# Grouping the narrow products of a fused filter, feed-forward and slot-routing kernel on one core

## The chip, the core and the metric

One core of a Trainium2 chip runs the whole program. The metric is device time in microseconds of one execution. The kernel before takes 1836.76 us (median of three runs, 1835.94 to 1837.98).

## What is computed

Three layers follow each other on x of 8 x 3072 x 256, all in float32:

```python
X = np.fft.rfft(x, axis=1); Y = X * (filt_r + 1j * filt_i)
x = np.fft.irfft(Y, n=3072, axis=1).reshape(24576, 256)     # filter
h = np.maximum(x @ w_in, 0.0); x = h * h @ w_out            # 256 -> 2048 -> 256
logits = x @ phi                                            # 32 slots, 4 for each of 8 experts
d = softmax(logits, axis=0); slot_in = d.T @ x              # over all 24576 rows
slot_out = relu(slot_in @ w1[e]) @ w2[e]                    # per expert
out = softmax(logits, axis=1) @ slot_out
```

## The kernel before, in words

The 24576 rows go through the feed-forward layer in 48 chunks of 512 rows, six to a batch. A chunk is eight pairs; a pair is two 128-wide tiles of the hidden layer, each made by six full 128 x 128 products of 512 columns (`layer`, L594 to L596, into the PSUM banks `p0` and `p1`), then squared (`square`, L601, L603, L605) and turned (`turn_h`, L622). Time in the hand-written order counts in units of half a pair: a chunk is 16 units, and pair P runs from unit 2P to 2P + 2. `pair` fires, quarter by quarter, whatever stands in five lists (`dsp`, `mv`, `late`, `fft`, `w`, in this order) with a unit that has come. Functions that need PSUM banks wait for their turn until enough of five side banks (`s0` to `s4`) are free (`run_streams`, `takes`).

"Narrow" products use a part of the array, several at a time. There are six kinds:

- the logits (`logit`, L663, 128 x 32), fired by `pair` itself at units 1.5 and 9.5 of a chunk: 16 instructions each time
- the slots product of the chunk before (`slot_in`, L794, 128 x 32, 32 instructions) at unit 9.5, added into a running sum by `accum` (L855, L856)
- the inverse transform over n1 of the rows of the next chunk (`mm_y`, L514, 64 x 64, 64 instructions) at unit 9.5, then `even_y` (L522), `unfold` (L531), `lead_y` (L539) and `rest_y` (L546)
- the forward transform over n1 of a later batch (`mm_a`, L165, 64 x 64, 16 instructions, three per batch)
- the forward transform over n2 (`mm_b`, L299, 48 x 32, 64 instructions, four per batch), then the filter (`filt`, L310) and `join` (L319)
- the inverse over n2 (`mm_g2`, L218, 32 x 64, 64 instructions, four per batch), then `evac_g2` and `store_g2`

The first three stand in one stretch at unit 9.5: logits, slots, inverse over n1. The last three are placed by the table `when` (the units of `mm_a`, `mm_b` and `mm_g2` of a batch) and their loads by the table `LEAD`. In a batch from the fourth on, `mm_g2` and one `mm_a` stand at units 1.5 (behind the logits), one `mm_b` as well, and three `mm_b` and two `mm_a` stand at unit 6, alone among full products. All loads and stores but a few go through SP's queue in the order written. The last batches' transforms are done before the last six chunks.

Ahead of the chunks lies an opening of some 55 us (its own put list, `put0`): batch 0's transforms with the x loads (`load_u`), the conversion of 64-bit weights on VectorE (`conv`), and the first input tile `gi`. Behind them lies the expert stage and the output loop (L1403 to L1423), 48 steps that write 512 KB each.

Of the kernel before, what the change touches and what calls it, by code (L numbers as in the profile page):

```python
# [6 lines left out]
F32 = mybir.dt.float32  # L7
# [6 lines left out]
NB = 8  # L14
# [24 lines left out]
def body(tc, x, cA, cAf, fwp, fwd, ivp, inv, flt, cst, w_in, w_out, phi, w1, w2, out):  # L39
# [23 lines left out]
    def F(i):  # L63
        return ST["F0"] + ST["dF"] * i

    WI = [
        ([.26, .3], [[9.7, 9.9, 9.91, 9.92, 9.93, 9.94], [12.9, 13.3, 13.31, 13.32, 13.33, 13.34]], 20.4, 40.3),
        ([.35, .425], [[16.6, 17.1, 17.11, 17.12, 17.13, 17.14], [30.2, 40.4, 40.41, 40.42, 40.43, 40.44]], 47.2, 47.58),
        ([30.1], [[41, 46, 46.1, 46.2, 46.3, 46.4]], 47.3, W + .1),
# [5 lines left out]
         + [W + t for t in (7.45, 7.95, 7.5, 8, 8.95, 9)]),  # L75
        (W + 5.2, [W + 9.3, W + 9.6, W + 10.2, W + 11, W + 11.5, W + 12.1]
         + [W + t for t in (13.95, 14.45, 14, 14.5, 15.45, 15.5)]),
# [43 lines left out]


    def fft_events(b, pl, put, TA, TB, TG, n, st):
        xv = x[b].rearrange("(p n) d -> p n d", n=N2)
# [21 lines left out]

        def load_u(u):
            sl, n = divmod(2 * u, 4)
            st["x", sl] = st["big"][sl // 4][:, sl % 4]
            sync.dma_start(out=st["x", sl][:, n:n + 2], in_=xv[:, 2 * u:2 * u + 2, :])  # L150

# [203 lines left out]
        def store_g(i):  # L355
# [4 lines left out]
            for r in range(2):  # L360
                (act if i == 6 and r else sync).dma_start(
                    out=gv[i % 6, r], in_=st["go", i][64 * r:64 * r + 8]
                )

        def store_rest(nm, lo, hi):
# [10 lines left out]
        def load_ca():  # L376
            vec.memset(st["wz"], 0.0)
            act.dma_start(out=st["ca"], in_=cAf)
# [8 lines left out]
        if b == 0:  # L387
# [8 lines left out]
            for u in range(12):  # L396
                put((.2, .21, .22, .23, .24, .25, .27, .28, .29, .31, .33, .34)[u], load_u, u)
            put(.32, load_k, C_ID, C_SS)
            put(.46, load_k, C_I, C_ID)
# [9 lines left out]
            for i in range(8):  # L409
                put((.38, .4, .42, .44)[i] if i < 4 else F(i - 4) + 2.6, load_f, i)  # L410
                T = (16.8, 17.2, 20, 22.4, 24.9, 25.3, 27.4, 27.8)[i]
                for s in range(2):
                    put(T + .1 * s, mm_t, i, s)
                    put(T + .3 + .1 * s, evac_t, i, s)
                put(F(i) - 1.2, mm_b, i)
                for r in range(2):
                    put(F(i) + 1.25 * r, filt, i, r)
                    if i < 7:
                        put(F(i) + 1.3 + 1.25 * r, join, i, r)
                put((29.85, 32.3, 34.75, 37.2, 39.9, 41.5, 44.6, 40.5)[i], mm_g, i)  # L420
                T = (31.1, 33.6, 36.1, 38.6, 41.2, 44.7, 45.9, 42.4)[i]
                for c in range(4):
                    put(T, evac_g, i, c)
                put(T + 1.25, store_g, i)
            return

        for s, (TL, TF, T) in enumerate(TA):
            put(TL, load_x, s)
            for k in range(2):
                put(TF + k, fold_x, s, k)  # L430
                for g in range(2):
                    put(T + 0.5 + (0 if T % 16 == 6 else 0.5) * k, evac_a, s, k, g)
                put(T + 2 + 0.5 * k, store_a, s, k)
            put(T, mm_a, s)
        LW, LV, LF, LS = n["lead"]
        for j in range(4):
            T = TB[j]
            for k in range(2):
                i = 2 * j + k
                put(T - LW[j], load_w, i)  # L440
                put(T, mm_b, i)
                for r in range(2):
                    put(T + 0.5 + 2 * k + r, filt, i, r)
                    put(T + 1 + 2 * k + r, join, i, r)
# [4 lines left out]
            put(T, mm_g2, j)  # L449
            for c in range(4):  # L450
                put(T + 0.5 + 0.5 * (c // 2), evac_g2, j, c)
            put(T + 3, store_g2, j)

    def out_events(b, st, late):

        def load_g(g):
            if b + g:
                t = G["mlp"].tile([128, 4, D], F32, tag="gin", name="gin", bufs=2)
                src, o = (st["G1"], 0) if (b, g) == (0, 1) else (st["G"], 4 * g - 8 * (b == 0))
                sync.dma_start(out=t, in_=src[:, o:o + 4, :])  # L460
            else:
                t = scratch("gi", 1, [128, 4, D])
                sync.dma_start(out=t[0:96], in_=st["Gu"])
                sync.dma_start(out=t[96:128], in_=st["Gz"])
            st["gi", g] = t

# [37 lines left out]
        def mm_y(g):  # L504
            t = st["gi", g]
            st["y", g] = p = [side() for e in range(2)]
            for a in range(4):
                for k in range(2):
                    for e in range(2):
                        for d in range(2):  # L510
# [6 lines left out]
                                start=True, stop=True, skip_group_check=True, tile_position=(64 * e, 64 * d),  # L517
                            )

        def even_y(g):  # L520
# [27 lines left out]
        for g in range(NCB):  # L548
            if 6 * b + g not in (0, 1, 6):
                T = 96 * b + 16 * g - 6.5  # L550
                late(max(T - 19.5, 13.5), load_g, g)
                late(T, mm_y, g)
                late(T + 0.5, even_y, g)
                late(T + 1, unfold, g, ALU.add)
                late(T + 1, unfold, g, ALU.subtract)
                for k in range(2):
                    late(T + 2 + 2 * k, lead_y, g, k)
                    late(T + 2.5 + 2 * k, rest_y, g, k)
                continue
# [138 lines left out]
    def dispatch_events(c, put):  # L698
# [87 lines left out]
        def slot_in():  # L786

            st["S"] = S = side()
            e, h = st["eT"], hd.pop(c)
            for t in range(4):  # L790
                for n in range(4):
# [4 lines left out]
                        start=(t == 0), stop=(t == 3), tile_position=(0, 32 * n),  # L796
                    )

        def slot_blocks():
# [91 lines left out]
        else:  # L891
# [3 lines left out]
            put(q + 4, expo)  # L895
            put(q + 4, turn_l)
            put(q + 5, rescale)
# [5 lines left out]
        else:  # L903
            put(q + 7.5, slot_in)
            put(q + 9, accum)
        put(q + 11, row_max)
# [47 lines left out]
    def conv(key, k, part=slice(0, 1024)):  # L954
# [11 lines left out]
        if k < 5:  # L966
            wst["s", key].pop(0)()
        else:
            e = gps if key[0] == "o" and key[1] else vec
            e.tensor_tensor(out=a, in0=a, in1=wst["e", key].bitcast(F32), op=ALU.add)  # L970

# [60 lines left out]
    def takes(fn, a):  # L1032
        if fn is conv_wo and a[1] in (6, 7, 10):
            return 1
        return take.get(fn.__name__, 0)

# [72 lines left out]
    with tc.manual_schedule():  # L1109
# [25 lines left out]
        for n in range(4):  # L1135
# [4 lines left out]
        LEAD = [  # L1140
            [[6.5, 6.5, 9.5, 9.5], [10, 7.5, 8, 10], [5, 6, 6.5, 6.5], [5.5, 10.5, 10, 10]],
            [[5.5, 7.5, 15.25, 15.25], [6.5, 12.5, 13.5, 13.5], [5, 5.5, 10, 10], [5.5, 13, 15.25, 15.25]],
            [[20.25] + [15.25] * 3, [13.5] * 4, [20.5, 10, 10, 10], [8, 15.25, 15.25, 15.25]],
        ]
# [8 lines left out]
        for b in range(1, NB):  # L1153
            st = {}
            if b == 1:
                when = ([(22, 24.5, 26.5), (24, 29, 33.5), (27.5, 32, 36.5)], [47, 54.5, 65.5, 76.5], [53, 61.5, 70.5, 81.5])
            elif b == 2:
                when = ([(-19, -15.5, -10), (-11, -7, -3), (-5.5, -3, 0)], [13.5, 22, 38, 54], [18.5, 33.5, 49.5, 65.5])
            else:
                when = ([(-41, -31, -26), (-28, -22.5, -14.5), (-22.5, -15.5, -10)], [1.5, 22, 38, 54], [17.5, 33.5, 49.5, 65.5])  # L1160
            fft_events(b, lambda: G["fft"], stream("fft", 96 * (b - 1)), *when, dict(f=3, u=8, c=2, lead=LEAD[min(b, 3) - 1]), st)
            out_events(b, st, late)
# [239 lines left out]

        obs = [w1t[n][:, 4 * D * h:4 * D * (h + 1)] for n in range(1, 5) for h in range(2)]  # L1403
        ops = 0
        for g in range(NG):
            b, o = divmod(g, N2 // 4)
            ov = out[b * N:(b + 1) * N, :].rearrange("(p n) d -> p n d", n=N2)
            ct = cts.pop(g)
            ob = obs[g % len(obs)].rearrange("p (a d) -> p a d", d=D)
            for h in range(2):  # L1410
                p = bank(("s0", "s1", "s2", "s3")[ops % 4]).rearrange("p (a d) -> p a d", d=D)
                ops += 1
                for a in range(2):
                    pe.matmul(p[:, a, :], ct[:, 2 * h + a, :], sr, start=True, stop=True)  # L1414
                if h == 0:
                    act.activation(out=ob[:, 0:2, :], in_=p, func=ACTF.Copy)
                else:
                    vec.tensor_copy(ob[:, 2:4, :], p)
                if g == 0:
                    sync.dma_start(out=ov[:, 2 * h:2 * h + 2, :], in_=ob[:, 2 * h:2 * h + 2, :])  # L1420
            if g:
                sync.dma_start(out=ov[:, 4 * o:4 * o + 4, :], in_=ob)
                go(*((turn, stack) if g == 1 else (turn, keep, stack)))  # L1423
# [154 lines left out]
```

## Time and profile before

| | us |
|---|---|
| median of three runs | 1836.76 |
| the profiled execution | 1835.65 |
| its span, first to last instruction | 1833.9 |
| PE busy | 1804.7 (98%) |
| VectorE, ScalarE, GpSimd busy | 1199.4, 1035.1, 781.2 |
| DMA queue of SP, share of 16 engines | 79.3% |

A row of the timeline gives the start in us from the span's start, the length, the engine, the line in the source, the tiles and how many instructions are merged. Matmuls overlap by their pipeline, so the time that one takes is read from start to start and not from its length. A row of the windows gives, for a stretch, the busy time of each engine with its instructions, the granted TensorE clock, the busy share of the DMA engines and GB/s.

### The profile page before, as it was taken

The page shows a single profiled execution, that of the slowest core. Times are in us where ns is not written, and L with a number is a line of the kernel's source. Part 1 is how long each engine was busy: PE and PEld are TensorE (multiplying, and loading weights), DVE is VectorE, ACT ScalarE, POOL GpSimd, SP SyncE. Part 2 cuts the span into 40 slices and gives each one's busy share as a digit, 9 for nine tenths or more (in the row PEclk, how much of TensorE's full clock was granted, in tenths as well). Part 3 has the DMA queues.
Part 4 walks back from the last instruction along what each step waited for, and adds up shares of the span by engine and source line. Part 5 has one row for each costly group of instructions (what it writes and reads, how often), then busy time and mean ns, then how long its engine had stood idle before and what let it go on. Part 6 is the DMA issues. An engine that isn't in the chain of part 4 may idle for free.

```text
span 1833.9 us, 42128 instructions
## 1 busy us (share of the span) xinstructions
PE 1804.7 (98%) x16326; PEld 1192.0 (65%) x16326; DVE 1199.4 (65%) x2264; ACT 1035.1 (56%) x1930; POOL 781.2 (43%) x815
## 2 busy tenths in 40 slices
PE   9999999999999999999999999999999999999986
PEld 7666666666666666666666666666666676666555
DVE  7956666676666666666667666666576756565568
ACT  6755555555555564555655565556555565555545
POOL 4144553444444534544444444444354533333234
PEclk9999999999999999999999999999999999999999
DMA  9779889888877896887978798788878666675989
GB/s 314 214 186 279 259 234 259 258 223 227 248 213 200 227 275 182 232 238 211 260 210 222 204 259 230 194 234 222 259 201 234 193 179 176 171 205 151 304 307 378
DMA packets 239846, 425.03 MB, mean 232 GB/s; under 512 B 25888, under 2 KB 95136, under 8 KB 239648
## 3 DMA queue, kind: packets, MB, share of 16 engines
q1 hardware_dynamic: 238776, 421.13, 79.3%
q8 instruction: 130, 2.13, 0.5%
q10 hardware_dynamic: 728, 1.15, 0.2%
q14 instruction: 68, 0.56, 0.1%
q0 software_dynamic: 144, 0.07, 0.0%
HBM read 151.71 MB, written 77.59 MB: 125 GB/s over the span
## 4 chain that ended last, share of the span: by engine, by line
PE 95%; DVE 2%; issue 1%; DMA 1%; ACT 1%; POOL 0%; SPq 0%; ACTq 0%; DVEq 0%; POOLq 0%
PE p L594 21%; PE p L596 19%; PE p L595 19%; PE L L663 10%; PE sd L794 9%; PE sd L299 3%; PE sd L218 3%; PE sd L514 3%; PE sd L165 2%; DVE ct L1212 1%; PE pt L1201 1%; PE sd L265 1%; PE pt L1414 1%; PE sd L339 1%; PE sd L724 1%
## 5 line engine op out<-in xcount | busy, mean ns | idle before, releaser
L605 POOL TENSOR_TENSOR h<-h 128x512 f32<-128x512 f32 x375 | 392.5, 1047 | 735.4 <-ACT h L601 681.5
L601 ACT ACTIVATE h<-p 128x512 f32<-128x512 f32 x768 | 459.0, 598 | 332.6 <-PE p L596 319.6
L622 DVE STREAM_TRANSPOSE hT<-h 128x512 f32<-128x512 f32 x736 | 485.2, 691 | 243.9 <-ACT h L603 230.9
L594 PE MATMUL p<-xo,wiH 128*128 128x512 f32 x1534 | 621.9, 405 | 0.2
L596 PE MATMUL p<-xo,wiL 128*128 128x512 f32 x1534 | 605.9, 395 | 0.6 <-DVE wiL L980 0.6
L595 PE MATMUL p<-xo,wiH 128*128 128x512 f32 x1534 | 605.1, 394 | 0.0
L594 PEld LDWEIGHTS p<-xo,wiH 128*128 128x128 f32 x1534 | 288.1, 188 | 123.6 <-issue 44.3
L596 PEld LDWEIGHTS p<-xo,wiL 128*128 128x128 f32 x1534 | 288.3, 188 | 69.8 <-DVE wiL L980 1.1
L595 PEld LDWEIGHTS p<-xo,wiH 128*128 128x128 f32 x1534 | 288.6, 188 | 60.7
L603 ACT ACTIVATE h<-h 128x512 f32<-128x512 f32 x393 | 248.4, 632 | 12.5
L319 POOL TENSOR_TENSOR u<-u 128x256 f32<-128x256 f32 x224 | 160.4, 738 | 110.9 <-DVE u L310 110.9
L663 PE MATMUL L<-h,wf 128*32 128x512 f32 x1536 | 186.9, 599 | 0.4 <-ACT h L603 0.4
L531 DVE TENSOR_TENSOR gin<-gin,sd 128x512 f32<-128x512 f32 x90 | 61.8, 687 | 179.5 <-ACT gin L522 177.9
L522 ACT ACTIVATE gin<-sd 128x512 f32<-128x512 f32 x45 | 26.9, 598 | 256.4 <-PE sd L514 256.4
L794 PE MATMUL sd<-hd,eT 128*32 128x512 f32 x1472 | 166.4, 592 | 0.0
L310 DVE TENSOR_TENSOR u<-sd,f 128x512 f32<-128x512 f32 x240 | 152.7, 674 | 10.4 <-PE sd L299 9.0
L794 PEld LDWEIGHTS sd<-hd,eT 128*32 128x32 f32 x1472 | 48.0, 110 | 109.9 <-issue 106.1
L546 POOL TENSOR_TENSOR xo<-gin,xo 128x512 fp32r<-128x512 f32 x90 | 119.2, 1324 | 0.0
L713 DVE TENSOR_TENSOR lo<-L,lp 128x512 fp32r<-128x512 f32 x47 | 32.3, 687 | 114.5 <-ACT lp L712 114.5
L228 ACT ACTIVATE f<-sd 128x512 f32<-128x512 f32 x112 | 61.1, 610 | 80.0 <-PE sd L218 80.0
L663 PEld LDWEIGHTS L<-h,wf 128*32 128x32 f32 x1536 | 40.0, 109 | 93.9 <-issue 92.1
L156 POOL TENSOR_TENSOR f<-f 128x512 f32<-128x512 f32 x42 | 54.3, 1294 | 67.4 <-DVE u L155 48.1
(162 smaller groups left out, 1599.5 us busy)
## 6 DMA issues: line engine op xcount, KB each, us to landing
hd<-hT SPq DMA_DIRECT2D x736, 256.0 KB
f<-flt SPq DMA_DIRECT2D x28, 1024.0 KB
gin<-G SPq DMA_DIRECT2D x47, 512.0 KB
out<-w1t SPq DMA_DIRECT2D x47, 512.0 KB
f<-x SPq DMA_DIRECT2D x84, 256.0 KB
S<-f SPq DMA_DIRECT2D x42, 512.0 KB
f<-S SPq DMA_DIRECT2D x112, 192.0 KB
G<-f SPq DMA_DIRECT2D x112, 192.0 KB
```

Source lines behind the costliest of these rows:

```text
L310: vec.tensor_tensor(out=u, in0=p.rearrange("p (h d) -> p h d", d=D), in1=f[:, 2 * r + k:2 * r + k + 1, :].to_broadcast([128, 2, D]), op=AL ...
L319: gps.tensor_tensor(out=a[:, h, :], in0=a[:, h, :], in1=b[:, 1 - h, :], op=ALU.add if h else ALU.subtract)
L546: gps.tensor_tensor(out=lo, in0=st["gi", g][:, k::2, :], in1=hi, op=ALU.subtract)
L594: pe.matmul(p, wh, x[:, 0, kk, :], start=(kk == 0), stop=False)
L595: pe.matmul(p, wh, x[:, 1, kk, :], start=False, stop=False)
L596: pe.matmul(p, wl, x[:, 0, kk, :], start=False, stop=(kk == 1))
L601: act.activation(out=h, in_=p, func=ACTF.Relu, scale=2.0 ** -8)
L603: act.activation(out=h, in_=h, func=ACTF.Square)
L605: gps.tensor_tensor(out=h, in0=h, in1=h, op=ALU.mult)
L622: vec.transpose(hT[c, f // 8][:, f // 4 % 2, :, o:o + 128], h2[P, k].rearrange("p (b t) -> p b t", b=4))
L663: pe.matmul(lg[c][32 * n:32 * n + 32, :], wf[:, f, :], h2.pop((P + n // 2, n % 2)), start=(f < 4), stop=(f >= FT - 4), tile_position=(0, 3 ...
L794: pe.matmul(S[32 * n:32 * n + 32, :], e[:, 32 * t:32 * t + 32], v, start=(t == 0), stop=(t == 3), tile_position=(0, 32 * n),)
```

## The change

A new table `WHEN` moves the transforms: from the fourth batch on, all `mm_b` and two `mm_a` stand at unit 1.5 of a chunk, and all `mm_g2` and one `mm_a` at unit 9.5 (batches 2 and 3 in part). A chunk with a transform at 9.5 is in the set `mid`: there `mm_y` goes ahead of the slots product (unit 9.49, list `dsp`) and takes the bank `p1` and one side bank, and the slots product takes the bank `p0`, so that four side banks are left for the transform. So the order there is logits, `mm_y`, slots, transform. `accum` comes right behind, evacuations are spread over more units, and the leads of the loads are shorter. `turn_l` comes 2.5 units later.

In the opening, the warm-up is fourteen instructions of 128 columns (seven products) and not two of 512, x comes in two loads of 256 KB and five of 512 KB, the first weight conversions stand earlier, one weight load stands later, and `gi` is loaded in four parts, the first ahead of the last stores. A conversion on GpSimd is cut in two. In the output loop eight rows a partition are written at once (1 MB) instead of four, and one copy in eight moves from VectorE to ScalarE.

```diff
-        ([.26, .3], [[9.7, 9.9, 9.91, 9.92, 9.93, 9.94], ...
+        ([.215, .25], [[6.3, 7, 7.01, 7.02, 7.4, 7.41], ...
...
+    WHEN = [
+        ([(22, 24.5, 26.5), (24, 29, 33.5), (27.5, 32, 36.5)], [47, 54.5, 65.5, 76.5], [53, 57.5, 73.5, 81.5]),
+        ([(-19, -15.5, -10), (-11, -7, -3), (-5.5, -3, 1.5)], [13.5, 22, 33.5, 49.5], [18.5, 25.5, 41.5, 57.5]),
+        ([(-45, -38.75, -30.5), (-38.75, -29, -22.5), (-25.5, -22, -14.5)], [1.5, 17.5, 33.5, 49.5], [9.5, 25.5, 41.5, 57.5]),
+    ]
+    mid = {
+        int((96 * (b - 1) + T) // 16)
+        for b in range(1, NB) for ta, _, tg in [WHEN[min(b, 3) - 1]] for T in [v[2] for v in ta] + tg if T % 16 == 9.5
+    }
...
-            put(0.05, warm, st["wz"], 1)
+            put(0.05, warm, st["wz"][:, 0:128], 7)
...
+            put(46.5, load_gi, sync, 0, "Gu", 0, 64)
...
+                late = T % 16 == 9.5
-                    put(T + 0.5 + (0 if T % 16 == 6 else 0.5) * k, evac_a, s, k, g)
+                    put(T + (2 + 2 * k if late else 0.5 + (0 if T % 16 == 6 else 0.5) * k), evac_a, s, k, g)
...
-            st["y", g] = p = [side() for e in range(2)]
+            st["y", g] = p = [G["ps"].tile([128, CH], F32, tag="p1", name="y") if 6 * b + g - 1 in mid else side(), side()]
...
-                late(T, mm_y, g)
+                if 6 * b + g - 1 in mid:
+                    stream("dsp")(T - 0.01, mm_y, g)
+                else:
+                    late(T, mm_y, g)
...
+                    t = T + (1 if 6 * b + g - 1 in mid else 2 + 2 * k)
+                    late(t, lead_y, g, k)
...
-            st["S"] = S = side()
+            st["S"] = S = G["ps"].tile([128, CH], F32, tag="p0", name="S") if c + 1 in mid else side()
...
-            put(q + 9, accum)
+            put(q + (7.6 if c + 1 in mid else 9), accum)
...
-                when = ([(-41, -31, -26), (-28, -22.5, -14.5), (-22.5, -15.5, -10)], [1.5, 22, 38, 54], [17.5, 33.5, 49.5, 65.5])
...
+            if g > NG - 3:
+                r = slice(4 * (g % 2), 4 * (g % 2) + 4)
+                sync.dma_start(out=ov[:, r, :], in_=ob[:, r, :])
+            elif g > 1 and g % 2:
+                sync.dma_start(out=ov, in_=ob)
```

## Rows read from the trace of the kernel before

**Rows 1.** The page, busy time of each engine over the span.

```profile
PE 1804.7 (98%) x16326; PEld 1192.0 (65%) x16326; DVE 1199.4 (65%) x2264; ACT 1035.1 (56%) x1930; POOL 781.2 (43%) x815
```

**Rows 2.** Windows mid-run: busy us of PE, PEld, DVE, ACT, POOL.

```profile
500.00:1000.00 500.00, 500.00 (x4633) 329.48 (x4617) 324.61 (x620) 280.93 (x521) 226.58 (x235) 1.00 0.80 224
```

**Rows 3.** Timeline of PE, the stretch at unit 9.5 of one chunk.

```profile
934.12 0.39 PE L596 MATMUL p<-xo,wiL 128*128 128x512 f32 x1
934.44 1.92 PE L663 MATMUL L<-h,wf 128*32 128x512 f32 x16
936.18 3.62 PE L794 MATMUL sd<-hd,eT 128*32 128x512 f32 x32
939.72 1.16 PE L514 MATMUL sd<-cst_t,gin 64*64 64x64 f32 x64
940.82 0.50 PE L594 MATMUL p<-xo,wiH 128*128 128x512 f32 x1
941.15 0.39 PE L595 MATMUL p<-xo,wiH 128*128 128x512 f32 x1
941.38 0.40 PE L596 MATMUL p<-xo,wiL 128*128 128x512 f32 x1
```

**Rows 4.** Timeline of PE, transforms behind the logits at unit 1.5 (L218, then L299).

```profile
951.88 0.40 PE L596 MATMUL p<-xo,wiL 128*128 128x512 f32 x1
952.21 1.92 PE L663 MATMUL L<-h,wf 128*32 128x512 f32 x16
954.06 1.98 PE L218 MATMUL sd<-u,iv 32*64 32x256 f32 x64
...
956.32 0.39 PE L595 MATMUL p<-xo,wiH 128*128 128x512 f32 x1
...
918.55 0.40 PE L596 MATMUL p<-xo,wiL 128*128 128x512 f32 x1
...
922.95 0.39 PE L595 MATMUL p<-xo,wiH 128*128 128x512 f32 x1
```

**Rows 5.** Timeline of PE, full products round L299, L165 and L663 alone.

```profile
822.95 0.40 PE L596 MATMUL p<-xo,wiL 128*128 128x512 f32 x1
...
825.50 0.39 PE L595 MATMUL p<-xo,wiH 128*128 128x512 f32 x1
...
893.82 0.40 PE L596 MATMUL p<-xo,wiL 128*128 128x512 f32 x1
...
896.37 0.39 PE L595 MATMUL p<-xo,wiH 128*128 128x512 f32 x1
...
1638.31 0.40 PE L596 MATMUL p<-xo,wiL 128*128 128x512 f32 x1
...
1640.83 0.39 PE L595 MATMUL p<-xo,wiH 128*128 128x512 f32 x1
```

**Rows 6.** Timeline of the weight loads, a wait of a lone L165.

```profile
283.70 0.20 PEld L165 LDWEIGHTS sd<-f,ca_t 64*64 64x64 f32 x4 [0.76 <-POOL f L156]
```

**Rows 7.** Timelines of VectorE and ScalarE behind the stretch of rows 3.

```profile
941.61 1.41 DVE L531 TENSOR_TENSOR gin<-gin,sd 128x512 f32<-128x512 f32 x2 [4.90 <-ACT gin L522]
942.94 0.74 DVE L855 SCALAR_TENSOR_TENSOR ac<-ac,sc,sd 128x512 f32<-128x512 f32 x1
...
946.48 0.62 ACT L539 ACTIVATE xo<-gin 128x512 fp32r<-128x512 f32 x1
```

**Rows 8.** Windows of the opening, columns as in rows 2.

```profile
10.00:20.00 10.00, 9.30 (x83) 9.09 (x82) 7.09 (x13) 7.88 (x14) 0.00 (x0) 1.00 1.05 395
20.00:30.00 10.00, 10.00 (x178) 7.28 (x177) 9.90 (x18) 7.16 (x14) 6.58 (x10) 1.00 1.01 375
```

**Rows 9.** Timeline of PE, the end of the opening.

```profile
48.02 4.46 PE L471 MATMUL sd<-cst_t 128*128 128x416 f32 x12 [1.31 <-ACT x L352]
53.40 2.02 PE L478 MATMUL sd<-cst_t,gi 128*128 128x128 f32 x16 [0.93 <-DMA gi<-Gz]
```

**Rows 10.** Windows of the output loop, columns as in rows 2.

```profile
1780.00:1800.00 20.00, 17.04 (x125) 14.48 (x126) 19.32 (x33) 14.03 (x32) 11.54 (x16) 1.00 1.02 405
```

More of the change, by code (lines that the diff above doesn't have):

```diff
@@ L145, in load_x, with load_u @@
                     )
-        def load_u(u):
-            sl, n = divmod(2 * u, 4)
+        def load_u(sl, n, m):
             st["x", sl] = st["big"][sl // 4][:, sl % 4]
-            sync.dma_start(out=st["x", sl][:, n:n + 2], in_=xv[:, 2 * u:2 * u + 2, :])
+            sync.dma_start(out=st["x", sl][:, n:m], in_=xv[:, 4 * sl + n:4 * sl + m, :])
         def fold_x(s, k):
@@ L363, in store_g, with load_gi @@
                 )
+        def load_gi(eng, o, nm, lo, hi):
+            if o + lo == 0:
+                st["gi", 0] = scratch("gi", 1, [128, 4, D])
+            eng.dma_start(out=st["gi", 0][o + lo:o + hi], in_=st[nm][lo:hi])
+        st["load_gi"] = load_gi
         def store_rest(nm, lo, hi):
@@ L395, in fft_events @@
             put(0.04, lambda: vec.memset(st["AT"][:, :, :, N2:], 0.0))
-            for u in range(12):
-                put((.2, .21, .22, .23, .24, .25, .27, .28, .29, .31, .33, .34)[u], load_u, u)
-            put(.32, load_k, C_ID, C_SS)
+            for n in range(2):
+                put(.2 + .01 * n, load_u, 0, 2 * n, 2 * n + 2)
+            for sl in range(1, 6):
+                put((.22, .23, .24, .27, .28)[sl - 1], load_u, sl, 0, 4)
+            put(.26, load_k, C_ID, C_SS)
             put(.46, load_k, C_I, C_ID)
@@ L449, in fft_events @@
             put(T, mm_g2, j)
+            late = T % 16 == 9.5 and b > 1
             for c in range(4):
-                put(T + 0.5 + 0.5 * (c // 2), evac_g2, j, c)
-            put(T + 3, store_g2, j)
+                put(T + ((2, 4, 5, 6)[c] if late else 0.5 + 0.5 * (c // 2)), evac_g2, j, c)
+            put(T + (6.5 if late else 3), store_g2, j)
     def out_events(b, st, late):
@@ L460, in load_g @@
                 sync.dma_start(out=t, in_=src[:, o:o + 4, :])
[L461 to L465, printed above, removed]
+                st["gi", g] = t
+                return
+            st["load_gi"](act, 0, "Gu", 64, 96)
+            st["load_gi"](sync, 96, "Gz", 16, 32)
+            st["load_gi"](sync, 96, "Gz", 0, 16)
         def warm():
@@ L518, in mm_y @@
                             )
+        mm_y.takes = lambda g: 1 if 6 * b + g - 1 in mid else 2
         def even_y(g):
@@ L556, in out_events @@
                 for k in range(2):
-                    late(T + 2 + 2 * k, lead_y, g, k)
-                    late(T + 2.5 + 2 * k, rest_y, g, k)
+                    t = T + (1 if 6 * b + g - 1 in mid else 2 + 2 * k)
+                    late(t, lead_y, g, k)
+                    late(t + 0.5 + (0.5 * k if t == T + 1 else 0), rest_y, g, k)
                 continue
@@ L797, in slot_in @@
                     )
+        slot_in.takes = lambda: 0.5 if c + 1 in mid else 1
         def slot_blocks():
@@ L895, in dispatch_events @@
             put(q + 4, expo)
-            put(q + 4, turn_l)
+            put(q + (6.5 if c < NCH - 2 else 4), turn_l)
             put(q + 5, rescale)
@@ L968, in conv @@
         else:
-            e = gps if key[0] == "o" and key[1] else vec
-            e.tensor_tensor(out=a, in0=a, in1=wst["e", key].bitcast(F32), op=ALU.add)
+            e = wst["e", key].bitcast(F32)
+            if key[0] == "o" and key[1]:
+                for o in (slice(0, 512), slice(512, 1024)):
+                    gps.tensor_tensor(out=a[:, o], in0=a[:, o], in1=e[:, o], op=ALU.add)
+            else:
+                vec.tensor_tensor(out=a, in0=a, in1=e, op=ALU.add)
     def conv_wi(j, k, part):
@@ L1034, in takes @@
             return 1
+        if fn.__name__ in ("mm_y", "slot_in"):
+            return fn.takes(*a)
         return take.get(fn.__name__, 0)
@@ L1154, in body @@
             st = {}
[L1155 to L1159, printed above, removed]
-                when = ([(-41, -31, -26), (-28, -22.5, -14.5), (-22.5, -15.5, -10)], [1.5, 22, 38, 54], [17.5, 33.5, 49.5, 65.5])
-            fft_events(b, lambda: G["fft"], stream("fft", 96 * (b - 1)), *when, dict(f=3, u=8, c=2, lead=LEAD[min(b, 3) - 1]), st)
+            fft_events(b, lambda: G["fft"], stream("fft", 96 * (b - 1)), *WHEN[min(b, 3) - 1], dict(f=3, u=8, c=2, lead=LEAD[min(b, 3) - 1]), st)
             out_events(b, st, late)
@@ L1401, in body @@
         go(keep, stack, stack)
-        obs = [w1t[n][:, 4 * D * h:4 * D * (h + 1)] for n in range(1, 5) for h in range(2)]
+        obs = [w1t[n].rearrange("p (a d) -> p a d", d=D) for n in range(1, 5)]
         ops = 0
         for g in range(NG):
-            b, o = divmod(g, N2 // 4)
-            ov = out[b * N:(b + 1) * N, :].rearrange("(p n) d -> p n d", n=N2)
+            b, o = divmod(8 * (g // 2), N2)
+            ov = out[b * N:(b + 1) * N, :].rearrange("(p n) d -> p n d", n=N2)[:, o:o + 8, :]
             ct = cts.pop(g)
-            ob = obs[g % len(obs)].rearrange("p (a d) -> p a d", d=D)
+            ob = obs[g // 2 % len(obs)]
             for h in range(2):
```

33 lines of the change are left out of this document (17 added, 16 removed).

## The prediction, made before the changed kernel ran

> **What bounds the kernel now.** I read the page first: PE is busy 1804.7 of 1833.9 us [rows 1]. Then the windows of the middle: in 500 us PE is busy 500.00, at granted clock 1.00, while VectorE has 325 and ScalarE 281 [rows 2]. So there time changes only if PE's own chain gets shorter, or if something new stops it. The number of products does not change, therefore what matters is the steps between them, which I read from the timeline of PE, start to start.
>
> A full product follows the one before by 0.23 (941.15 to 941.38) [rows 3]. Into a narrow stretch the step is 0.32 (934.12 to 934.44), 0.09 more; the first step among full products behind it is 0.33 (940.82 to 941.15), 0.10 more [rows 3]. Within a stretch, the logits take 1.74 when the slots follow, which have the same shape [rows 3], and 1.85 when another shape follows [rows 4]: 0.11 for leaving a shape. The slots take 3.54 with that 0.11, so 3.43 for eight rounds of four; the logits' four rounds should take 1.715 and take 1.74, so entering a shape costs some 0.03 [rows 3].
>
> **The change, part by part.**
>
> *Lone transforms that move behind the logits.* With its two full steps, L299 alone takes 2.55 (822.95 to 825.50) and L165 alone 2.55 (893.82 to 896.37) [rows 5]; less 0.46 for two ordinary steps, 2.09 each. Behind the logits L299 costs 4.40 [rows 4] less the logits alone, 2.52 [rows 5]: 1.88. A transform that gives up its own stretch saves 0.21. Counting units in the two tables: batches 4 to 8 give up five lone ones each (three L299, two L165), batch 3 three, batch 2 two L218: 30 x 0.21 = -6.3 us.
>
> *The inverse over n1 ahead of the slots.* Now logits and slots are one shape in a row. With L514 between them the array leaves the first shape (0.11) and enters it again (0.03): +0.14. `mid` has 30 chunks (two in batch 2, three in batch 3, five in each later one): +4.2 us. The trace of before has no step from L514 to L794. At best coming back is free (0), at worst it costs twice (0.28, +8.4). I take 0.14: the 0.11 for leaving is read directly where L218 follows the logits [rows 4], and with it the slots' and the logits' rounds come out alike [rows 3]. L218 moved from unit 1.5 to the end of this stretch costs 1.92 (4.44 [rows 4] less 2.52 [rows 5]) in either place: 0. Together: -2.1 us, between -6.3 and +2.1.
>
> The Trainium skill, TensorEngine Tiling (Array Packing), Key Properties, says that a change of tiling mode drains TensorE. Counted by that alone, a batch from the fourth on has 46 changes of mode before (six stretches of three, six of three, five lone ones of two) and 46 after (five of five, one of three, six of three), and nothing would be won. The trace agrees that each change costs, but not that all cost the same: between narrow shapes it is 0.14, while a lone stretch pays 0.09 + 0.03 + 0.11 + 0.10 = 0.33 for its two.
>
> *Waits.* One lone L165 of batch 3 waited 0.76 for GpSimd's fold [rows 6]; its unit is now 1.5 later and behind the logits, so -0.8 (0 if another wait takes the place).
>
> *New waits in the stretch.* `mm_y` writes `p1` and must wait until the last tile there is read; the logits cover that for 1.85 [rows 4], and an evacuation of this size takes 0.6 (L539, 0.62 [rows 7]). The next pair's first product writes `p0` and waits for `accum`, 0.74 [rows 7]; the transform behind the slots covers it for 1.9 [rows 4]. Without that cover each chunk would lose 0.74. Behind `accum` stand on VectorE the two `unfold` (1.41 together [rows 7]), and behind these on ScalarE both `lead_y` (2 x 0.62 [rows 7]), now ahead of the next pair's first relu. From the slots' end that makes 0.74 + 1.41 + 1.24 = 3.4; the first tile of the next pair is done at 1.9 + 0.1 + 6 x 0.23 = 3.4, and its bank is wanted again 1.4 later. With 0.6 for the relu there is some 0.8 of slack. A fold of x that falls into this order would use it up, in about one chunk a batch. I set +0.6 us for this and for late loads (0 to +9). SP's order changes as well: loads stand nearer to their use, and the first move of a chunk's turned tiles waits for the slots' end, which comes 1.1 later (L514, 939.72 to 940.82 [rows 3]); DMA has a share of 0.80 there [rows 2], so I add nothing.
>
> *Opening.* VectorE idles 2.9 us between 10 and 20 and 0.1 between 20 and 30 [rows 8], where it becomes the bound with the filter products. A conversion moved ahead of these lets them begin when PE delivers; but PE is busy 9.30 of the ten before [rows 8] and can hardly deliver earlier. I take -0.7 (0 to -2.9). The warm-up's fourteen instructions, at 0.11 each (9.30 us for 83 [rows 8]) or twice that, last 1.6 to 3.1 us and lie beside the first x load: 0; it costs up to +1 if the weights, now ahead of most of x, delay x. At the end PE's warm-up lasts until 52.48, and the last tile's product begins at 53.40 behind the load of Gz [rows 9]: loading in parts can win at most 0.92; I take -0.7. Together -1.4 (+1.0 to -2.5).
>
> *Output loop.* DMA's share is 1.02 at 405 GB/s [rows 10]: transfers bound it, though VectorE is close (19.32 of 20). So the copies moved to ScalarE bring nothing by themselves. Larger pieces may: with mostly 2 KB rows the engines give 395 at 1.05 [rows 8], that is 376 at full share, 87 ns for 2 KB; with 4 KB rows 405 at 1.02, 397, or 165 ns. By the same line 8 KB take 321 ns, 408 GB/s: 2.8% of 62 us (25.2 MB at 405), -1.7. The first whole megabyte waits for two steps, once, +0.5 (estimate; a step is 1.3, 512 KB at 405). Together -1.2 (0 to -1.9).
>
> **Sum.** -2.1 - 0.8 + 0.6 - 1.4 - 1.2 = -4.9 on the profiled 1835.65: 1830.8. The median of the runs, 1836.76, stands 1.1 above that execution, so I forecast 1831.9.
>
> **Rivals.**
> 1. *Coming back to the slots' shape costs nothing*, because L514's last rounds are short and the slots' weights can be loaded beside them. For: L514 has the shortest rounds. Against: no row shows a change of shape that is free. Then 4.2 more is won: 1827.7. Chance 0.13.
> 2. *All changes of shape cost alike in the new order*, so that the regrouping is worth 0, with the ends of the run as forecast: 1834.0, within 0.2%. The rule of the page named above leads here. Smaller gains at the ends lead to the same place. Chance 0.20.
> 3. *The change doesn't do what it says*: where fewer than four side banks are free at unit 9.5, the transform slips by half a unit among full products and is alone again, while the 0.14 stays. All 30 would give 1831.9 + 6.3 = 1838.2, also within 0.2%. Against: by the units all filter products of the chunk and `turn_l` stand before 9.5. Chance 0.07.
> 4. *Slower: ScalarE's relu stands behind `lead_y`.* If VectorE reaches `accum` late or carries more in that order than I reckoned, every us beyond the slack of 0.8 is a us of PE, in 30 chunks. It decides from 0.3 beyond the slack (30 x 0.3 = 9, more than the gain of 4.9 by over 3.7); with 0.7 beyond, 1831.9 + 21 = 1853. For: the chain is in the order by hand. Against: VectorE is idle 4.90 ahead of its `unfold` in the same place now [rows 7]. Late transfers would have the same sign. Chance 0.15.
>
> **How the numbers follow.** The forecast's own case (1829.5 to 1833.1) has 0.45. About 0.2% (3.7 us) is what a measurement of this kernel can tell from no change: 1833.1 and 1840.4 are the bounds. Faster: 0.45 + 0.13 = 0.58. Same: 0.20 + 0.07 = 0.27. Slower: 0.15. The range reaches from just under rival 1 to rival 3 and a little of rival 4: 1827.2 to 1839.0, which leaves out some 2 in 10.
>
> **What the profile after would show.** Stretches at unit 9.5 in the order L663, L514, L794, L218 or L165, from the last full product to the second one behind it 9.1 (7.03 + 0.14 + 1.92) in 30 chunks; the slots some 3.57 long in place of 3.54; no lone L299 or L165 in batches 4 to 8. No wait of PE on `accum` or on ScalarE behind such a stretch; the last tile's product 1.4 earlier than 53.40; the output loop at 410 to 415 GB/s. It would be wrong if full products behind the stretch wait, if slots begin late for want of turned tiles, or if the opening's x comes late.

## The result and the profile after

The changed kernel takes 1859.34 us (median of four runs, 1858.87 to 1861.02) beside 1836.44 for the kernel before on the same chip: ratio 1.0125, interval 1.0111 to 1.0139, 22.9 us slower. The forecast was 1831.9 with 1839.0 as its upper end; it was wrong, in size and in sign. The profiled execution took 1861.02, its span is 1859.2, against 1835.65 and 1833.9 before: 25.4 to explain.

First the page of the changed kernel, busy time of each engine:

```profile
PE 1820.6 (98%) x16338; PEld 1236.9 (67%) x16338; DVE 1200.0 (65%) x2252; ACT 1045.6 (56%) x1942; POOL 780.8 (42%) x818
```

and its window in the middle (busy us of PE, PEld, DVE, ACT, POOL, then clock, DMA share, GB/s):

```profile
500.00:1000.00 500.00, 499.15 (x4545) 341.05 (x4544) 323.51 (x613) 278.12 (x512) 226.06 (x234) 1.00 0.82 221
```

PE is as busy as before, at the same clock [rows 1, 2], but in the same 500 us it gets through 4545 instructions in place of 4633. So most of the loss looks like work, not like waiting, and the share of busy time can't show it; it has to be read from start to start. I added up PE's steps, start to start, over all its rows in both timelines:

| part of the span | before | after | difference |
|---|---|---|---|
| opening, up to the first `layer` product | 55.3 | 60.2 | +4.9 |
| first to last `layer` product | 1674.7 | 1695.8 | +21.1 |
| behind the last one | 104.0 | 103.2 | -0.8 |

In the main part the regrouping itself did what it should: the first steps behind stretches fall from 156 to 126 (-3.3), and the stretches with the merged transforms, in the old order, are 1.9 cheaper (experiment 1 against before), together -5.2. Against that stand 30 stretches with `mm_y` ahead of the slots, +18.2 compared with the same stretches in the other order (experiment 1); waits between full products (steps of over 0.4 among products of 512 columns, counted by what they have beyond 0.23), +6.2; and +1.9 of small steps. One such stretch, from PE's timeline of the changed kernel, in the place that answers to [rows 3]:

```profile
952.06 0.39 PE L624 MATMUL p<-xo,wiL 128*128 128x512 f32 x1
952.38 1.93 PE L691 MATMUL L<-h,wf 128*32 128x512 f32 x16
954.23 0.27 PE L536 MATMUL y<-cst_t,gin 64*64 64x64 f32 x2
...
955.32 4.15 PE L822 MATMUL S<-hd,eT 128*32 128x512 f32 x32
959.40 1.98 PE L227 MATMUL sd<-u,iv 32*64 32x256 f32 x64
961.31 0.50 PE L622 MATMUL p<-xo,wiH 128*128 128x512 f32 x1
961.65 0.39 PE L623 MATMUL p<-xo,wiH 128*128 128x512 f32 x1
```

From the last full product to the second behind it 9.59; the median of the 25 with an inverse over n2 is 9.61, the forecast was 9.09. Logits (1.85), `mm_y` (1.09) and transform (1.91) have the lengths of before. The slots take 4.08 (955.32 to 959.40) in place of 3.54. So of the 0.65 that the new order costs here, 0.11 is the logits' (1.85 in place of 1.74, the forecast's price of leaving a shape) and 0.54 the slots'. The same line shows both lengths in one kernel. Here are the groups of L822 by line (busy us, mean ns, idle before), with bank S (the 30 chunks) and with a side bank (16 chunks where the slots follow the logits):

```profile
L822 PE MATMUL S<-hd,eT 128*32 128x512 f32 x960 | 125.0, 593 | 0.0
L822 PE MATMUL sd<-hd,eT 128*32 128x512 f32 x512 | 57.9, 592 | 0.0
```

125.0 / 30 is 4.17 a chunk, 57.9 / 16 is 3.62. One instruction takes the same, so it is the overlap that differs. Windows over the first half microsecond, for the slots' line alone, count how many of its products are running in the changed kernel:

```profile
955.30:955.35 0.05, 0.03 (x1) 0.03 (x1) 1.00 0.22 82
955.35:955.45 0.10, 0.10 (x2) 0.10 (x4) 1.00 0.00 0
955.45:955.60 0.15, 0.15 (x2) 0.07 (x3) 1.00 0.07 27
955.60:955.70 0.10, 0.10 (x3) 0.08 (x2) 1.00 0.01 0
955.70:955.80 0.10, 0.10 (x4) 0.06 (x2) 1.00 0.00 0
```

and in the kernel before:

```profile
936.17:936.22 0.05, 0.04 (x4) 0.04 (x4) 1.00 0.00 0
```

Before, the four column tiles start within 0.02 and run in step. Behind `mm_y` they start one after the other over 0.45. From there on a round takes 0.43 in either case, but for the first and the last behind `mm_y` (up to 0.53), so the lag never closes: it is paid once, at the end, when the last tile finishes.

### The profile page after: what moved, and what is told of

It is laid out like the page before. It is cut to its first block, busy times and chain, and to the rows that moved or that the text cites. A ratio compares the mean times of both kernels' runs of the same rounds, so it can differ in the third digit from the quotient of the medians.

```text
span 1859.2 us, 41843 instructions
## 1 busy us (share of the span) xinstructions
PE 1820.6 (98%) x16338; PEld 1236.9 (67%) x16338; DVE 1200.0 (65%) x2252; ACT 1045.6 (56%) x1942; POOL 780.8 (42%) x818
## 4 chain that ended last, share of the span: by engine, by line
PE 89%; DVE 4%; DMA 2%; ACT 2%; issue 1%; SPq 1%; POOL 0%; ACTq 0%; DVEq 0%
PE p L622 19%; PE p L624 18%; PE p L623 18%; PE L L691 9%; PE S L822 7%; PE sd L308 3%; PE sd L822 3%; PE sd L227 3%; PE sd L174 1%; PE y L536 1%; PE sd L536 1%; DVE ct L1242 1%; PE pt L1231 1%; PE pt L1444 1%; DMA f<-x 1%
## 5 line engine op out<-in xcount | busy, mean ns | idle before, releaser
L650 DVE STREAM_TRANSPOSE hT<-h 128x512 f32<-128x512 f32 x736 | 490.9, 694 | 321.9 <-ACT h L631 302.2
L629 ACT ACTIVATE h<-p 128x512 f32<-128x512 f32 x768 | 458.2, 597 | 322.7 <-PE p L624 303.1
L631 ACT ACTIVATE h<-h 128x512 f32<-128x512 f32 x393 | 248.4, 632 | 12.5
L563 ACT ACTIVATE xo<-gin 128x512 fp32r<-128x512 f32 x90 | 53.1, 622 | 162.8 <-DVE gin L555 162.8
L822 PE MATMUL S<-hd,eT 128*32 128x512 f32 x960 | 125.0, 593 | 0.0
L165 POOL TENSOR_TENSOR f<-f 128x512 f32<-128x512 f32 x42 | 54.2, 1291 | 100.1 <-DVE u L164 86.4
L822 PEld LDWEIGHTS S<-hd,eT 128*32 128x32 f32 x960 | 70.5, 109 | 29.3 <-issue 1.2
L885 DVE SCALAR_TENSOR_TENSOR ac<-ac,sc,S 128x512 f32<-128x512 f32 x30 | 22.4, 747 | 98.0 <-PE S L822 98.0
L237 ACT ACTIVATE f<-sd 128x512 f32<-128x512 f32 x112 | 64.6, 588 | 15.9 <-PE sd L227 15.9
```

The costliest lines, as they stand in the source:

```text
L629: act.activation(out=h, in_=p, func=ACTF.Relu, scale=2.0 ** -8)
L631: act.activation(out=h, in_=h, func=ACTF.Square)
L650: vec.transpose(hT[c, f // 8][:, f // 4 % 2, :, o:o + 128], h2[P, k].rearrange("p (b t) -> p b t", b=4))
L822: pe.matmul(S[32 * n:32 * n + 32, :], e[:, 32 * t:32 * t + 32], v, start=(t == 0), stop=(t == 3), tile_position=(0, 32 * n),)
```

## The experiments

Theory A: the slots are slow because they come straight behind the 64 x 64 products and their column tiles (the four 128 x 32 parts of the array that work side by side) lose step. Rivals: the bank `p0` or traffic at that moment (B), or waits that are not steps (C).

**1. `mm_y` behind the slots again, all else as changed.**

```diff
-                    stream("dsp")(T - 0.01, mm_y, g)
+                    stream("dsp")(T, mm_y, g)
```

> The changed kernel with one thing put back: in the 30 chunks of `mid` the inverse over n1 (`mm_y`) stands behind the slots again, so logits, slots, `mm_y`, transform; banks, lone transforms, opening and output loop stay as changed. Theory A (the slots are slow because they start straight behind the 64x64 products, their four column tiles out of step): the slots go from 4.15 back to about 3.55, the stretch from 9.6 to about 9.1, 30 x 0.5 = 15 us less, 1844 (1840 to 1847, the lower end if the waits of PE on ScalarE go too). Theory B (the slots are slow because they write bank p0 or because of traffic at that time): they stay at 4.1 and the time at 1859. Theory C (waits, not steps, carry the loss): 1855 or more.

Measured 1837.99, ratio 1.0002 (0.9993 to 1.0011): order alone carries some 22 of the 22.9. The stretch in PE's timeline of this kernel:

```profile
940.03 0.40 PE L624 MATMUL p<-xo,wiL 128*128 128x512 f32 x1
940.36 1.92 PE L691 MATMUL L<-h,wf 128*32 128x512 f32 x16
942.10 3.62 PE L822 MATMUL S<-hd,eT 128*32 128x512 f32 x32
945.64 0.27 PE L536 MATMUL y<-cst_t,gin 64*64 64x64 f32 x2
...
946.74 1.98 PE L227 MATMUL sd<-u,iv 32*64 32x256 f32 x64
948.65 0.50 PE L622 MATMUL p<-xo,wiH 128*128 128x512 f32 x1
948.99 0.39 PE L623 MATMUL p<-xo,wiH 128*128 128x512 f32 x1
```

8.96 in place of 9.61, and the slots 3.54 although they still write `p0`: A holds, B falls. 8.96 is also what the prediction's terms give without the price of coming back (7.03 + 1.92 = 8.95). With a forward transform over n1 behind it the stretch is 8.77 in place of 9.59 (five chunks): in the old order `mm_y` and that transform, which have one shape, stand side by side. The gain is larger than I expected because waits go as well: those between full products fall from 8.5 to 4.3 us (2.3 in the kernel before).

**2. The order alone, put into the kernel before.**

```diff
-                late(T, mm_y, g)
+                stream("dsp")(T - 0.01, mm_y, g)
```

> The kernel before with one thing changed: `mm_y` ahead of the slots in all 44 chunks where they share a stretch, side banks for all of it. Theory A (order alone makes the slots slow): slots 4.1 in place of 3.54, with the return to their shape some 0.65 a chunk, 44 x 0.65 = 28 us more, 1865 (1858 to 1868). The prediction's own price (0.14 for the return): 1842.6. Theory B (bank p0 is the cause): 1842 or less, slots at 3.55.

Measured 1875.35, ratio 1.0197 (1.0177 to 1.0217), 36 us more and above A's 1858 to 1868. One stretch of this kernel in PE's timeline:

```profile
1031.07 0.39 PE L596 MATMUL p<-xo,wiL 128*128 128x512 f32 x1
...
1034.34 4.25 PE L794 MATMUL sd<-hd,eT 128*32 128x512 f32 x32
1038.52 0.51 PE L594 MATMUL p<-xo,wiH 128*128 128x512 f32 x1
1038.87 0.39 PE L595 MATMUL p<-xo,wiH 128*128 128x512 f32 x1
```

The 44 stretches go from 7.04 to a median of 7.80, +0.76 a chunk or 33 us, with side banks for everything; that is beyond the 0.65 of A and five times the prediction's 0.14. A further 4.8 is one wait in batch 1 on VectorE's `lo`, which I didn't follow up; behind it the granted clock is 0.50 from 178.1 to 184.8.

**3. One small full product between `mm_y` and the slots.**

```diff
+            if c + 1 in mid:
+                pe.matmul(S[:, 0:64], cI, cI[:, 0:64], start=True, stop=True, skip_group_check=True)
```

> The changed kernel with one small 128x128 product of 64 columns put between `mm_y` and the slots in the 30 chunks; its result is written over by the slots. It needs the whole array, so all four column tiles are free at the same moment behind it. Theory A (lost common phase): slots back at about 3.55, the product itself costs 0.15 to 0.3, so the stretch gets 0.2 to 0.4 shorter in spite of more work: 1847 to 1853. Theory A' (it is not the phase, but the slots' loads that compete with something of that stretch) or B (bank p0): slots stay at 4.1 and the product comes on top, 1863 to 1868.

Measured 1858.49, ratio 1.0117 (1.0097 to 1.0137): no gain. PE's timeline says why:

```profile
951.56 0.43 PE L819 MATMUL S<-cst_t 128*128 128x64 f32 x2
951.93 3.85 PE L824 MATMUL S<-hd,eT 128*32 128x512 f32 x32
955.71 1.98 PE L227 MATMUL sd<-u,iv 32*64 32x256 f32 x64
```

The slots fall to 3.78 (951.93 to 955.71): three of their tiles now start together and one 0.25 later (0.20 to 0.26 in most chunks). But the product costs 0.37 itself. So the lag depends on what runs just ahead, as A says, while all four in step, as I expected, and with it the saving, didn't come.

**4. The slots at the end of the stretch, behind the transform.**

```diff
-        slot_in.takes = lambda: 0.5 if c + 1 in mid else 1
+        slot_in.takes = lambda: 0 if c + 1 in mid else 1
...
-            put(q + 7.5, slot_in)
+            (stream("w") if c + 1 in mid else put)(q + 7.5, slot_in)
```

> The changed kernel with the slots at the end of the stretch in the 30 chunks: logits, `mm_y`, transform, slots. Theory A (any other narrow shape ahead of the slots makes their four column tiles start apart): the slots' four first products start over some 0.4 to 0.5, slots near 4.1 also behind the transform; on top PE waits for `accum` 0.75 and more behind the stretch, 30 x 0.75 = 22: some 1880. Rival D (only the short 64x64 products do it): slots at 3.55, and the same wait: 1865.

One execution: 1913.56. PE's timeline:

```profile
389.72 0.47 PE L227 MATMUL sd<-u,iv 32*64 32x256 f32 x8
...
391.64 3.73 PE L822 MATMUL S<-hd,eT 128*32 128x512 f32 x32
396.21 0.50 PE L622 MATMUL p<-xo,wiH 128*128 128x512 f32 x1 [0.84 <-DVE ac L885]
```

The slots' group is 3.73 long; behind the short 64 x 64 products it was 4.15, behind the logits 3.62. So it isn't any other narrow shape that does it: rival D was right on the step, and my theory as worded there was too wide. Nor is it the shape 64 x 64: in five of the 30 chunks `mm_a` stands just ahead of the slots, which has that shape but 512 columns an instruction in place of 64, and there all four tiles start together (a window over the slots' first 0.05 us, then their row):

```profile
465.28:465.33 0.05, 0.05 (x4) 0.05 (x8) 1.00 0.00 0
465.28 3.64 PE L822 MATMUL S<-hd,eT 128*32 128x512 f32 x32
```

So that shape alone doesn't set the tiles apart; the lag goes with the 64 columns an instruction. One stretch of experiment 2 shows that these are not the only way to it: the last slots stand right behind the logits, but their operand `eT` comes late, PE stands still for 0.15, and the tiles start over 0.47:

```profile
1759.11 4.30 PE L794 MATMUL sd<-hd,eT 128*32 128x512 f32 x32 [0.15 <-DVE eT L770]
```

The totals of both theories were far too low. The order makes PE wait for `accum` in all 30 chunks (25.7 us together; the prediction reckoned 0.74 each if that cover were gone) and for ScalarE's relu 13 times (8.7); the transform stops four times (7.0), and the granted clock is 0.50 from 796.4 to 799.7 and from 1096.8 to 1103.5, behind two of these stops. The transform behind the slots is indeed the cover that the prediction named.

**5. The opening.** Whole old opening in the changed kernel; then, in the kernel before, only the first part (x, weights, warm-up, conversions), and only the loads of `gi`:

```diff
-            put(0.05, warm, st["wz"], 1)
+            put(0.05, warm, st["wz"][:, 0:128], 7)
...
-            for u in range(12):
-                put((.2, .21, .22, .23, .24, .25, .27, .28, .29, .31, .33, .34)[u], load_u, u)
...
+            for n in range(2):
+                put(.2 + .01 * n, load_u, 0, 2 * n, 2 * n + 2)
+            for sl in range(1, 6):
+                put((.22, .23, .24, .27, .28)[sl - 1], load_u, sl, 0, 4)
...
+            put(46.5, load_gi, sync, 0, "Gu", 0, 64)
...
-                sync.dma_start(out=t[0:96], in_=st["Gu"])
...
+            st["load_gi"](act, 0, "Gu", 64, 96)
```

> The changed kernel with the whole opening of the kernel before (order of x and weights, warm-up, conversions, gi in one load). Theory: the first product of the main part comes at 55.3 in place of 60.2 and nothing behind it changes, 4.9 less, 1854.4 (1853 to 1856). Rival: the later start of the main part is given back later, because the transforms of the next batch wait for loads anyway: 1858 to 1860.

> The kernel before with only the first part of the changed opening: weights ahead of most of x, x in 512 KB pieces, seven short warm-up products, the conversion of the first weights moved ahead; gi stays one load of Gu and one of Gz. Theory: x comes later, as in the changed kernel's trace, where PE waits 2.00 for x and the filter products begin 2.5 later; the warm-up ahead of the last tile starts near 50.8 in place of 48.0 and the main part begins near 58.0: 1839 (1838 to 1840). Rival: the start of the main part is set by the loads of gi, not by PE's work ahead of them, so 55.3 and 1836.5.

> The kernel before with only the loads of gi in parts (64 rows of Gu early, 32 rows by ScalarE's queue, Gz in two halves). Theory: the load of Gu's rows 64 to 96 on ScalarE's queue is the last to land, as in the changed kernel, and the last tile's product waits longer: the main part begins 1 to 2.1 later, 57, and 1838 (1837 to 1839). The prediction's -0.7: main part begins at 54.6, 1835.7.

Measured: 1855.76 (1.0094, 1.0079 to 1.0109), against 1.0125 for the whole change, so 0.31% or some 5.7 less; first part alone 1.0016 (1.0006 to 1.0025), +2.9; `gi` alone 1.0012 (1.0002 to 1.0021), +2.2. Both are losses, if barely clear of noise, and together come near the 5.7. Their profiled executions show less of it: the main part begins at 56.4 and 56.8, where I expected 58.0 and 57, and 55.3 in the kernel before. PE's timeline of the changed kernel:

```profile
9.56 10.83 PE L274 MATMUL sd<-ca,x 128*128 128x128 f32 x80 [2.00 <-DMA x<-x]
...
57.36 3.15 PE L500 MATMUL sd<-cst_t,gi 128*128 128x128 f32 x16 [2.07 <-DMA gi<-Gu]
```

of the changed kernel with the old opening:

```profile
53.51 2.02 PE L491 MATMUL sd<-cst_t,gi 128*128 128x128 f32 x16 [1.00 <-DMA gi<-Gz]
```

of the kernel before with the first part only:

```profile
9.56 9.25 PE L264 MATMUL sd<-ca,x 128*128 128x128 f32 x80 [1.72 <-DMA x<-x]
```

and of the kernel before with `gi` in parts only:

```profile
54.92 2.02 PE L486 MATMUL sd<-cst_t,gi 128*128 128x128 f32 x16 [2.27 <-DMA gi<-Gz]
```

PE waits 1.7 to 2.0 for x, now that x comes in pieces of 512 KB with weights ahead of most of it (which of the two does it wasn't tried), and for `gi` in four parts over 2 us instead of 0.9 [rows 9]. Which part it waits for last differs: Gu in the changed kernel, Gz in the kernel before, where I had expected Gu. The clock comes on top in the changed kernel. Its window just behind the wait for x:

```profile
10.00:13.60 3.60, 3.60 (x20) 3.60 (x19) 2.40 (x4) 0.61 (x1) 0.00 (x0) 0.53 1.03 397
```

0.53 of 2.4 GHz is close to the lower of the two levels, 1.2 GHz in place of 2.4, behind a wait of 2 us in which PE did nothing. Between 57.5 and 62, behind the wait for `gi`, it is 0.62, so that the last tile's sixteen instructions take 3.15 and not 2.02. Behind the waits of 1.72 and 2.27 in the two kernels with half of the change it is 1.00. So it differs from one execution to another: with the changed opening the main part began at 57.6 to 60.2 in five kernels' profiles, with the old one at 55.3 to 56.7 in seven.

**6. The output loop, in the kernel before.**

```diff
+                if h == 0 or g % 4 == 3:
+                    act.activation(out=ob[:, r, :], in_=p, func=ACTF.Copy)
...
-                    vec.tensor_copy(ob[:, 2:4, :], p)
...
+            elif g > 1 and g % 2:
+                sync.dma_start(out=ov, in_=ob)
```

> The kernel before with only the changed output loop (stores of 1024 KB, more copies on ScalarE). The prediction's -1.2: from the last full product of the layer to the end 102.7 in place of 103.95. From the changed kernel's trace: 103.2, -0.7. Either is within the error of the whole time, 1835.5 to 1836.5; the part behind the last full product tells.

Measured 1836.86, ratio 0.9998 (0.9989 to 1.0008): nothing that the whole time can show. In the trace the part behind the last `layer` product is 103.1 in place of 104.0; but over all profiles it is 103.6 to 104.0 with the old loop (four) and 103.1 to 103.9 with the new one (ten), so the gain may be nearer 0.4. Window of this loop in this kernel, to be held against [rows 10]:

```profile
1780.00:1800.00 20.00, 16.57 (x128) 14.44 (x126) 16.89 (x28) 15.77 (x36) 11.02 (x16) 1.00 0.99 407
```

407 GB/s at 0.99 is 411 at full share, where before it was 397; but the share fell by 0.03, and half a per cent of rate is what was left.

**7. `lead_y` later.** In about one chunk a batch (7 of the 30) the changed kernel shows rival 4 of the prediction. First VectorE's and ScalarE's rows behind such a stretch, then PE's:

```profile
676.81 0.69 DVE L164 TENSOR_TENSOR u<-f 128x512 f32<-128x512 f32 x1
677.41 1.40 DVE L555 TENSOR_TENSOR gin<-gin,sd 128x512 f32<-128x512 f32 x2
678.84 1.15 ACT L563 ACTIVATE xo<-gin 128x512 fp32r<-128x512 f32 x2 [6.33 <-DVE gin L555]
679.90 0.58 ACT L629 ACTIVATE h<-p 128x512 f32<-128x512 f32 x1
682.65 0.50 PE L622 MATMUL p<-xo,wiH 128*128 128x512 f32 x1 [0.41 <-ACT h L629]
```

A fold of x (L164) stands ahead of `unfold` on VectorE, so `lead_y` comes late, the relu (L629) behind it later still, and PE's step is 0.81 (681.84 to 682.65). The edit puts `lead_y` back to units 11.5 and 13.5:

```diff
-                    t = T + (1 if 6 * b + g - 1 in mid else 2 + 2 * k)
-                    late(t, lead_y, g, k)
...
+                    late(T + 2 + 2 * k, lead_y, g, k)
```

> The changed kernel with the two copies of `lead_y` (and `rest_y`) back at units 11.5 and 13.5 in the 30 chunks instead of both at 10.5; the rest as changed. Theory (rival 4 of the prediction, in about one chunk a batch): both copies stand ahead of the next pair's relu, and where a fold of x came between on VectorE, PE waits 0.81 between full products; with the copies later these waits go, 8.5 us of waits in the main part become some 2.5 to 4.5: 1854.5 (1853 to 1857). Rival: the relu then waits for something else of the same order, the waits stay: 1859.

Measured 1870.27, ratio 1.0174 (1.0156 to 1.0192): 9 us slower than the changed kernel. A clear miss. Steps of over 0.4 between full products go from 16 to 42; such a step follows in 29 of the 30 chunks. ScalarE's rows, then PE's, of this kernel:

```profile
824.73 0.62 ACT L563 ACTIVATE xo<-gin 128x512 fp32r<-128x512 f32 x1
825.25 0.58 ACT L237 ACTIVATE f<-sd 128x512 f32<-128x512 f32 x1
825.73 1.24 ACT L628 ACTIVATE h<-p 128x512 f32<-128x512 f32 x2
...
825.94 0.40 PE L623 MATMUL p<-xo,wiL 128*128 128x512 f32 x1
826.38 0.50 PE L621 MATMUL p<-xo,wiH 128*128 128x512 f32 x1
```

The changed kernel has the transform's evacuations (L237) at 11.5, 13.5, 14.5 and 15.5: at the old units each `lead_y` meets one, and two copies in a row hold up the relu in nearly every chunk, not in one a batch.

**8. What is left when order and opening are put back.** The changed kernel with the edits of 1 and the old opening:

> The changed kernel with `mm_y` behind the slots again in the 30 chunks and the old opening: what is left are the merged transforms, the waits and the output loop. Theory: the parts add: opening 55.3, main part 1673.7, end 103.2, span 1832.2 against 1833.9: 1834.5 (1833 to 1836). Rival: with the earlier start the transforms of the first batches wait for loads and give the 4.8 back: 1838.

Measured 1835.81, ratio 0.9993 (0.9984 to 1.0003): no difference that can be told. The parts don't simply add: beside experiment 1 (1.0002) the old opening gains only some 1.7 here, not 5.7, and the two intervals overlap. Its main part is 1675.5, that of the kernel before 1674.7 to 1676.0 in the four profiles with that main part. What the merged transforms save is given back: four of the stretches take 9.62 to 10.86 in place of 8.96 (in the longest the transform stops for 1.53 in its midst), and the waits between full products are 2.3 us longer than before. With the edit of 7 as well:

> The version that the runs so far point to: the changed kernel with `mm_y` behind the slots, the old opening, and `lead_y` at 11.5 and 13.5. Of the change there remain the merged transforms, the later units of their evacuations, the loads' leads and the output loop. Theory: the waits of 0.42 a batch and those of batches 1 and 2 go too, 4.6 become about 2.3, so 1672.5 to 1673.5 for the main part, 1833.5 (1831 to 1835.5), ratio 0.998. Rival: the waits stay, 1835.8, ratio 0.9993.

Measured 1845.76, ratio 1.0044 (1.0032 to 1.0057): some 9 us slower than without that edit, the collision of experiment 7 again. With the two copies at 10.5 and 12.5, between the evacuations:

```diff
+                    t = T + ((1 if 6 * b + g - 1 in mid else 2) + 2 * k)
```

> As the version with `mm_y` behind the slots and the old opening, but with the two copies of `lead_y` at units 10.5 and 12.5, between the evacuations of the transform (11.5, 13.5, 14.5, 15.5) and not upon them. Theory (copies at 11.5 and 13.5 were slow because each met an evacuation there): no steps of 0.44 between full products, and the wait of 0.42 a batch goes as well: main part 1673 to 1674.5, 1834.5 (1832.5 to 1836), ratio 0.9985. Rival (any second place for the copy delays the relu): main part above 1680, ratio 1.003 or more.

Measured 1835.79, ratio 0.9984 (0.9975 to 0.9993): the collision was the cause, for one unit's shift takes away all of the 0.6% between this and the version ahead. It is 2.9 us faster than the kernel before, at the edge of what can be told. The waits of 0.42 a batch stay in its trace, so the reason that I gave for those fell; and its profiled execution (1837.93) lies 2.1 above its median, so where the last 2 us come from I can't say.

## Why the prediction was wrong

- **The price of coming back to the slots' shape** (the return in the +0.14 a chunk, bounds 0 and 0.28) is the step that failed. The new order costs 0.65 where `mm_g2` follows, 0.82 where `mm_a` does, 0.76 in the kernel before. With 18.2 in place of 4.2 for the 30 chunks, the sum of -4.9 alone becomes +9. The sign failed here, and so did the range. Of the two terms in the 0.14, the 0.11 for *leaving* a shape came true (logits 1.85 in place of 1.74); the 0.03 for *entering* the slots' shape measures 0.54 (slots 4.08 in place of 3.54). That 0.03 was read off the logits behind a full product [rows 3] and used for the slots behind `mm_y`, and the bound was only the double of the sum, though the prediction itself says that no row shows L514 followed by L794. What was missing in the terms was the lag between column tiles. "Slower" had a chance of 0.15, all of it for waits and none for this price. The Trainium skill, TensorEngine Tiling (Array Packing), Key Properties, has each change of mode drain TensorE; the runs agree that a change costs but show that its price depends on the pair and its direction: from the slots' shape to that of the 64 x 64 products 0.11, back 0.54 behind `mm_y`. Logits, slots, `mm_y` (three changes with those at the ends) take 7.04; logits, `mm_y`, slots (four) 7.80, so that one change more is 0.76, while giving up a lone stretch, also one change, was worth some 0.2. Rival 2 (all changes alike) is excluded by that, and rival 1 (a free return) by the 0.54.
- **Lone transforms**: -5.2 of the forecast -6.3. Right, a little small.
- **The lone wait** (-0.8): the wait for GpSimd's fold is gone, but another took its place, as the bound 0 allowed. In the changed kernel the logits ahead of an `mm_a` wait 1.02 at 295 for GpSimd's square.
- **Rival 3** didn't happen: in the profile after no transform of batches 4 to 8 that was to move stands alone.
- **New waits**: +0.6 was forecast with 9 as the worst, +6.2 came. The mechanism of rival 4 is real, in about one chunk a batch as the sum assumed: in five batches a step of 0.81 in place of 0.23, 2.9 together, and in two earlier ones of 1.1, some 1.8. It doesn't decide; the order does, and it carries 4.2 of these 6.2 as well (experiment 1). The fold of x that "would use it up" did so.
- **Cover of `accum`**: right. No wait of PE on it in the changed kernel, 25.7 us once the cover is taken away.
- **Opening**: -1.4 with +1.0 as the worst; it is +4.9 in the profile, 5.7 by experiment 5, less by experiment 8. The late x was seen as "up to +1" and is 1.7 to 2; `gi` in parts was costed at a gain, and is a loss, without asking which of four loads lands last; the clock behind these waits wasn't in the sum.
- **Output loop**: -1.2 forecast, -0.8 and -0.9 in two profiles, some -0.4 over all of them, of no weight.

Put together: +18.2 for the order, +6.2 waits, +4.9 opening, +1.9 small steps, -5.2 merging, -0.8 at the end make 25.2 of 25.4.

## What to carry to other kernels

Where the busy share is 98% before and after, cost a reorder by steps from start to start, and where a pair of shapes never stands in that order in the trace, treat its price as unknown with a wide bound: one small run that swaps the pair settles it, while a neighbouring row does not. Products that share the array by columns did best here behind products of their own shape or behind long ones (256 or 512 columns); very short ones (64 columns) ahead of them set the tiles out of step for the whole group. And before a step is moved in an order by hand, look which steps of the same engine were moved to that very unit.

## What was not expected of the hardware

Four column tiles that start apart stay apart: behind `mm_y` (64 columns an instruction) the slots' tiles mostly start over 0.45 us, behind a full product of 64 columns three together and one mostly 0.20 to 0.26 later, behind `mm_g2` (256 columns) within 0.02 in 9 of 25 chunks and mostly one up to 0.25 late in the others, behind `mm_a` (512 columns) within 0.02, and behind the logits within 0.04, but for the one whose operand was late; the rounds then take 0.43 each wherever they started. That the weight loads of the first four stand close together, 0.41 to 0.43 ahead of the products, behind the logits and singly behind `mm_y` is in the rows. Loads so far ahead aren't needed for a start in step, for behind `mm_a` they stand right at the products and these start together; what spreads them behind `mm_y` wasn't tried. In the opening, the granted clock fell to its lower level behind waits of 2 us for loads, in some executions and not in others.
